# An attention and feed-forward kernel: units of three and two banks, score tiles for VectorE in a fourth row group, PV in pairs, and a finer split of the queries

## The chip, the cores and the metric

The kernel runs on one core of one Trainium2 chip. Times are device microseconds (us) of that core; a traced span is some 2 us shorter than the timed run it belongs to. The engines are called by name: TensorE (PE in the profile, with its weight loads PEld), VectorE (DVE), ScalarE (ACT), GpSimd (POOL) and SyncE (SP). There is only one core, so a "slow" state of a die cannot be told here; the runs that were timed in rounds were of the state fast, but for two of the kernel before (1024.07 and 1019.0 us), which the ratios leave out, and a kernel that was run once has the state unknown. Of those I compare stages of the trace, not the time. "Clock" is the share of its full speed that TensorE was granted: 1.00 is full, 0.50 is half ("lowered").

## The reference

One pre-norm transformer block on 2048 tokens of width 640, with 32 heads of 20, in bf16:

```python
def _A_ref(x, wqkv, wo):                      # attention
    qkv = (x @ wqkv) ... -> 3 x [B, H, S, Dh]
    scores = einsum("bhqd,bhkd->bhqk", q, k) * Dh ** -0.5
    p = softmax(scores)
    return einsum("bhqk,bhkd->bhqd", p, v) ... @ wo
def _B_ref(x, w_gate, w_up, w_down):          # feed-forward, width 1728
    return (gelu_tanh(x @ w_gate) * (x @ w_up)) @ w_down
h  = x + _A_ref(layernorm(x), wqkv, wo)
h2 = h + _B_ref(layernorm(h), w_gate, w_up, w_down)
```

The scores are 32 x 2048 x 2048 numbers. In the kernel they are 2048 tiles of 128 keys x 512 columns (512 queries of one head, or 256 queries of two key blocks), each the size of one PSUM bank. (PSUM is the memory that TensorE writes its results to; the kernel divides it into eight banks, 0 to 7.)

## The kernel before

Operations are recorded with a priority and their dependences, a small list scheduler fixes the order on each engine, and semaphores are derived from it. The order is therefore static, fixed when the program is built. Queries are handled in chunks; a "slot" is 64 tiles. The feed-forward of one chunk is background work for the attention of the next. (The code here is cut, and its comments are added.)

```python
CHUNKS = ((0, 512), (512, 512), (1024, 512), (1536, 256), (1792, 256))
D_SEL = (None, (6, 3), (6, 3), (4, 2), (4, 2))     # for VectorE: tiles per slot, and one in how many units
PV_QUADS = 1
WARM_WIN, WARM_MIN = 3.4, 0.40
...
# units of score tiles, by chunk: the banks of even and odd units
PAT = [((0, 1), (2, 3))] + [((0, 1, 2), (3, 4, 5))] * 2 + [((0, 1, 2), (3, 4))] * 2
BG  = [tuple(b for b in (7, 5, 4) if b not in PAT[c][0] + PAT[c][1]) for c in ...]   # background banks
```

A unit is two or three QK matmuls, each in its own 32-row group of TensorE, then one exponential on ScalarE over all its banks, then PV matmuls with four heads side by side in column groups ("a quad"), accumulated in bank 6. In some units of three the third tile goes to VectorE instead, which computes the exponential for a pair of tiles in integer and bf16 arithmetic:

```python
def d_exp(b, tile, prio):
    op("dve", I("tensor_scalar", v[...half...], PS[...bank...], EXP_MUL, -32000.0, ALU.mult, ALU.max), ...)
    if h == 0: return                       # wait for the second tile of the pair
    d(I("tensor_scalar", fi, v, 511, None, ALU.bitwise_and), ...)
    d(I("tensor_scalar", dw, fi, -1.0 / OCT, 1.0, ALU.mult, ALU.add), ...)
    d(I("tensor_tensor", dw, dw, fi, ALU.mult), ...)
    d(I("tensor_scalar", df, fi, -E1 / OCT, -E0, ALU.mult, ALU.add), ...)
    d(I("tensor_tensor", dw, dw, df, ALU.mult), ...)
    d(I("tensor_tensor", v, v, dw, ALU.add), ...)
    d(I("tensor_scalar", v, v, 0.25, 16256.0, ALU.mult, ALU.add), ...)
```

Where the scheduler finds TensorE idle and its use in the last 3.4 us below WARM_MIN, it puts in a matmul whose result nobody reads ("warm-up").

## Time and profile before

| | before |
|---|---|
| time, median of 3 runs | 1009.06 us (1006.16 to 1015.02) |
| traced span | 1011.4 us |
| exponentials on ScalarE | 802 for 1920 tiles; 128 tiles on VectorE |
| prologue / attention / tail | 43.3 / 925.3 / 42.8 us |
| clock 0.50 inside the attention | 8 periods, 51 us |

The lines that carry this are in the prediction below. Two things help in reading them. A row of busy time by stretch counts overlapping instructions once, so 96% for an engine says "nearly always something in flight", not "at its limit"; the limit is read from the spacing of starts. And the wait of an engine is worth something only on the path: TensorE idles before a QK because ScalarE still reads the banks (23.9 and 17.7 us in its list of waits), and that costs nothing while ScalarE sets the pace.

A bookkeeping that I use throughout: ScalarE's waits in the attention are the length of the stages, less 0.917 us for each two-bank and 1.345 us for each three-bank exponential, less the gelu interludes (9.15 us for 512 queries, 5.9 us for 256). Before, that leaves 21.3 us.

### The profile page before, as it was taken

To read this page: it belongs to the slowest core of one execution; us is meant where nothing else is said; L and a number is where in the kernel's file an instruction comes from. 1 tells how busy PE (TensorE), PEld (TensorE's weight loads), DVE (VectorE), ACT (ScalarE), POOL (GpSimd) and SP (SyncE) were. 2 spreads that over 40 slices of the span, in tenths; PEclk is the share of its full clock that TensorE was granted. 3 is DMA by queue.
4 is the path that set the end of the run, shared out by engine and by line. 5 is a ranking of instruction groups with operands and counts; after the bars stand their busy time and mean duration, and the time that the engine had idled before them with its cause. 6 is when DMAs were issued, how large, how long until landed. Compare 5 with 4: busy or idle time off the path is not lost.

```text
span 1011.4 us, 17239 instructions
## 1 busy us (share of the span) xinstructions
PE 912.7 (90%) x7392; PEld 321.1 (32%) x7392; DVE 642.6 (64%) x1319; ACT 936.9 (93%) x873; POOL 19.6 (2%) x42
## 2 busy tenths in 40 slices
PE   3999999999988788798998888889899989999988
PEld 2533322222222222222332222223333333334446
DVE  7744445555497887577669777576677645475542
ACT  3799999999999899989989999999999999999941
POOL 7000000000000000000000000000000000000000
PEclk9999999999998999899979999999999989999999
DMA  6000000000006100000010000000000000000000
GB/s 234 1 1 1 1 2 1 1 1 1 4 12 241 36 1 1 1 1 1 14 33 20 1 1 1 1 1 15 27 15 2 1 1 1 14 28 2 1 14 14
DMA packets 11820, 18.88 MB, mean 19 GB/s; under 512 B 672, under 2 KB 9824, under 8 KB 11744
## 3 DMA queue, kind: packets, MB, share of 16 engines
q1 hardware_dynamic: 11744, 17.78, 5.2%
q8 instruction: 58, 0.95, 0.4%
q14 instruction: 18, 0.15, 0.0%
HBM read 15.16 MB, written 2.62 MB: 18 GB/s over the span
## 4 chain that ended last, share of the span: by engine, by line
ACT 69%; PE 22%; DVE 6%; DMA 1%; POOL 1%; issue 1%; SPq 0%; POOLq 0%; DVEq 0%
ACT pts L305 49%; ACT rege L305 19%; PE ps L305 8%; PE ps L859 6%; PE ps L909 3%; PE ps L548 3%; DVE qt_all L305 3%; DMA rege<-in_A_wqkv_dram 1%; PE ps L512 1%; POOL regw L305 1%; DVE rege L305 1%; DVE rege L887 1%; DVE rege L898 1%; ACT L305 1%; PE ps L583 0%
## 5 line engine op out<-in xcount | busy, mean ns | idle before, releaser
L305 ACT ACTIVATE pts<-ps 128x1024 bf16<-128x1024 f32 (+1 forms) x590 | 650.3, 1354 | 13.4 <-PE ps L305 13.1
L305 PE MATMUL ps<-qt_all,kt_all 32*128 32x512 bf16 (+1 forms) x2560 | 316.2, 344 | 49.4 <-ACT pts L305 23.7
L305 ACT ACTIVATE rege<-ps 128x1536 bf16<-128x1536 f32 (+1 forms) x212 | 276.2, 1431 | 10.6 <-PE ps L305 10.3
L859 PE MATMUL ps<-rege,regw 128*128 128x512 bf16 (+2 forms) x700 | 169.8, 357 | 18.1 <-DVE rege L898 7.0
L305 PE MATMUL ps<-pts,v_all 128*21 128x512 bf16 (+1 forms) x1673 | 173.4, 350 | 0.3 <-ACT pts L305 0.2
L305 PEld LDWEIGHTS ps<-qt_all,kt_all 32*128 32x128 bf16 x2560 | 81.7, 91 | 279.2 <-ACT pts L305 164.6
L548 PE MATMUL ps<-regw 128*128 128x512 bf16 (+1 forms) x480 | 135.9, 363 | 3.2 <-DMA regw<-in_A_wqkv_dram 2.8
L305 DVE TENSOR_TENSOR qt_all<-qt_all 128x1024 bf16<-128x1024 bf16 (+1 forms) x160 | 110.0, 688 | 3.6
L305 PE MATMUL ps<-rege,v_all 128*21 128x512 bf16 (+1 forms) x807 | 99.6, 340 | 0.5 <-DVE osb L305 0.5
L859 PEld LDWEIGHTS ps<-rege,regw 128*128 128x128 bf16 (+1 forms) x700 | 59.9, 101 | 96.1 <-issue 45.5
L909 PE MATMUL ps<-regw,rege 128*128 128x320 bf16 x448 | 87.3, 307 | 1.3 <-DVE rege L877 0.8
L305 DVE TENSOR_SCALAR qt_all<-qt_all 128x1024 int16<-128x1024 int16 (+1 forms) x192 | 81.1, 422 | 4.5
L305 PEld LDWEIGHTS ps<-pts,v_all 128*21 128x21 bf16 x1673 | 43.1, 89 | 82.4 <-issue 80.5
L898 DVE TENSOR_TENSOR rege<-rege,ps 128x512 bf16<-128x512 bf16 (+1 forms) x49 | 33.6, 685 | 53.5 <-PE ps L859 53.3
L305 DVE TENSOR_SCALAR qt_all<-ps 128x512 int16<-128x512 f32 x64 | 44.0, 687 | 32.3 <-PE ps L305 32.1
L305 DVE TENSOR_SCALAR rege<-ps 128x512 int16<-128x512 f32 x64 | 43.9, 686 | 24.0 <-PE ps L305 23.5
L548 PEld LDWEIGHTS ps<-regw 128*128 128x128 bf16 x480 | 38.7, 99 | 61.8 <-issue 47.2
L909 PEld LDWEIGHTS ps<-regw,rege 128*128 128x128 bf16 x448 | 36.6, 98 | 45.9 <-issue 29.9
L887 DVE CAST rege<-ps 128x512 bf16<-128x512 f32 (+1 forms) x49 | 33.6, 686 | 22.4 <-PE ps L859 22.4
L572 DVE TENSOR_SCALAR kt_all<-ps,e 128x512 bf16<-128x512 f32 x28 | 21.0, 749 | 28.4 <-PE ps L548 28.3
L575 DVE CAST qt_all<-ps 128x512 bf16<-128x512 f32 x31 | 21.4, 689 | 25.9 <-PE ps L548 25.9
L913 DVE TENSOR_TENSOR rege<-ps,rege 128x320 bf16<-128x320 f32 x32 | 15.6, 488 | 34.0 <-PE ps L909 33.9
(78 smaller groups left out, 591.1 us busy)
## 6 DMA issues: line engine op xcount, KB each, us to landing
rege<-in_A_x_dram SPq DMA_DIRECT2D x4, 640.0 KB, 6.3
out_dram<-rege SPq DMA_DIRECT2D x16, 160.0 KB, 1.8
rege<-in_A_x_dram SPq DMA_DIRECT2D x14, 160.0 KB, 2.2
regw<-in_B_w_gate_dram SPq DMA_DIRECT2D x1, 2160.0 KB, 9.5
regw<-in_B_w_up_dram SPq DMA_DIRECT2D x1, 2160.0 KB, 14.6
regw<-in_B_w_down_dram SPq DMA_DIRECT2D x1, 2080.0 KB, 19.7
rege<-in_A_wqkv_dram SPq DMA_DIRECT2D x1, 1600.0 KB, 11.4
regw<-in_A_wqkv_dram SPq DMA_DIRECT2D x1, 800.0 KB, 13.1
```

What stands on the lines that cost most here:

```text
L305: return lambda eng: getattr(eng, method)(*args, **kwargs)
L512: op("pe", lambda eng, a=a: eng.transpose(bank16(bk, D)[:, 128 * a:128 * a + 128], src[:, a * 128:(a + 1) * 128], ident[:]), 0.055, prio, ...
L548: yield op("pe", lambda eng, l=l, r=r, k=k: eng.matmul(bank(bk, n), l, r, start=(k == 0), stop=(k == len(steps) - 1)), c_mm(n), prio, mode ...
L572: op("dve", lambda eng: eng.tensor_scalar(dst, bank(bk), e0[:, 0:1], None, ALU.add), c_dve(512) + 0.06, prio, reads=[key, "e0"], writes=[( ...
L575: op("dve", lambda eng: eng.tensor_copy(dst, bank(bk)), c_dve(512), prio, reads=[key], writes=[(nm, g, c)], rel=[bk])
L859: op("pe", lambda eng, a=a, f=f, fi=fi, mf=mf: eng.matmul(bank(bk)[0:mf, fi * nq:(fi + 1) * nq], w[:, a, f * 128:f * 128 + mf], hnT[:, a, ...
L887: cp.append(op("dve", lambda eng, bg=bg, fv=fv, m=m: eng.tensor_copy(fv, bank(bg)[0:m, :]), c_dve(512), p, reads=[kg], writes=[("ha", k)], ...
L898: hdone.append(op("dve", lambda eng, bu=bu, fv=fv, m=m: eng.tensor_tensor(fv, fv, bank(bu)[0:m, :], ALU.mult), c_dve(512), p, reads=[ku, ( ...
L909: op("pe", lambda eng, f=f, mf=mf, o=o, hf=hf, bk=bk: eng.matmul(bank(bk, 320), ha_f[0:mf, o:o + 128], wd[0:mf, f, hf * 320:(hf + 1) * 320 ...
L913: op("dve", lambda eng, bk=bk, tt=tt, hf=hf, i=i: eng.tensor_tensor(ob[:, i, hf * 320:(hf + 1) * 320], bank(bk, 320), h_sb[:, tt, hf * 320 ...
```

## The change

It aims at ScalarE, by giving VectorE more score tiles, and at TensorE, by fewer changes between its full, row-tiled and column-tiled forms. The core of the diff, cut and with comments added:

```diff
-WARM_WIN, WARM_MIN = 3.4, 0.40
+WARM_WIN, WARM_MIN = 3.4, 0.5
+PE_AGE = 1.5                      # scheduler: prefer a ready run of TensorE's present form
...
-CHUNKS = ((0, 512), (512, 512), (1024, 512), (1536, 256), (1792, 256))
+SIZES = (512, 512, 256, 256, 256, 256)
...
-PV_QUADS = 1
+PV_QUADS = 2
-PR, PR2 = 9, 6
+PR, PR2 = 12, 6
-D_SEL = (None, (6, 3), (6, 3), (4, 2), (4, 2))
+D_PER_SLOT = (4,6,8,8,8,8)
+D_FIRST, D_SPAN = 1, 16
...
-        PAT = [((0, 1), (2, 3))] + [((0, 1, 2), (3, 4, 5))] * 2 + [((0, 1, 2), (3, 4))] * 2
+        PAT = [((0, 1, 2), (3, 4))] * len(CHUNKS)
...
+            if xd:                                  # the VectorE tile of this unit
+                bd = Bank(*BG[slots[xd[0]][0]])     # a background bank, 7 or 5
+                qd = op("pe", [qk_mms(lambda: bank(bd), xd, kk) ...], 0.08,
+                        P_QK + 0.5, mode="row", ..., acq=[bd], after=[qk])
```

The rest moves buffers: the residual x is fetched straight into the accumulator tile, feed-forward buffers alternate between two halves for chunks of 256, and VectorE's scratch for chunk 0 lies in the feed-forward buffer.

## The prediction

> **What bounds the kernel now.** I read the page first, then cut the span into stages at the exponentials of each chunk of queries, then read the chain of waits for the spacing of exponentials, the timeline for the spacing of TensorE's runs, and the groups by shape for VectorE's share.
>
> The page's first part names two engines that could be the bound, and it cannot decide between them, because consecutive instructions overlap in it:
>
> ```profile
> PE 912.7 (90%) x7392; PEld 321.1 (32%) x7392; DVE 642.6 (64%) x1319; ACT 936.9 (93%) x873; POOL 19.6 (2%) x42
> ```
>
> The second view is the table of busy time by stretch. Its six rows are chunks 0 (512 queries), 1, 2 (512 each), 3, 4 (256 each) and the tail after the last exponential; after the stretch and its length come PE, PEld, DVE, ACT, POOL, the granted clock, DMA share and GB/s:
>
> ```profile
> 43.30:278.60 235.30, 234.26 (x1447) 68.64 (x1446) 115.75 (x208) 234.77 (x256) 0.00 (x0) 1.00 0.01 2
> 278.60:506.10 227.50, 193.91 (x1394) 59.43 (x1390) 170.40 (x340) 217.81 (x178) 0.00 (x0) 0.95 0.10 34
> 506.10:730.00 223.90, 195.33 (x1440) 62.49 (x1439) 162.85 (x325) 219.15 (x180) 0.00 (x0) 0.96 0.03 11
> 730.00:850.60 120.60, 113.66 (x1270) 39.87 (x1269) 77.17 (x161) 118.34 (x111) 0.00 (x0) 0.97 0.02 5
> 850.60:968.60 118.00, 113.39 (x1376) 49.18 (x1375) 67.86 (x142) 116.25 (x108) 0.00 (x0) 0.99 0.04 11
> 968.60:1011.40 42.80, 34.73 (x283) 24.61 (x279) 16.05 (x43) 8.21 (x13) 0.00 (x0) 1.00 0.04 12
> ```
>
> ScalarE is at 96 to 100% of every attention stage; VectorE has room everywhere. The true price of an exponential is its spacing in the chain, not its duration (1.23 and 1.60 us by shape):
>
> ```profile
> 43.36 209.09 ACT pts L305 x228
> ...
> 388.91 2.69 ACT rege L305 x2
> ```
>
> The first merged line is two-bank exponentials of chunk 0: 209.09/228 = 0.917 us each. The second is three-bank ones: 2.69/2 = 1.345 us. The difference, 0.428 us, is one 512-column tile; 0.917 - 2 x 0.428 = 0.061 us is the fixed cost. So merging units saves little, and taking a tile off ScalarE saves 0.428 us.
>
> The ScalarE sum for before: 1920 tiles x 0.428 + 802 exponentials x 0.061 = 821.8 + 48.9 = 870.7 us. The tanh-gelu interludes add 9.15 us for 512 queries (table load at 417.27, next exponential at 426.42) and 5.9 us for 256: 3 x 9.15 + 5.9 = 33.3. Prologue 43.3, tail 42.8. Together 990.1; the traced span is 1011.4, so 21.3 us are waits of ScalarE for TensorE, nearly all in chunks 1 to 4.
>
> Those waits sit beside a lowered clock. One of the places, in the timeline (ScalarE alone) and the table of stretches:
>
> ```profile
> 425.13 1.28 ACT L305 ACT_TABLE_LOAD   x1
> 426.42 2.37 ACT L305 ACTIVATE pts<-ps 128x1024 bf16<-128x1024 f32 x2
> 431.32 2.53 ACT L305 ACTIVATE rege<-ps 128x1536 bf16<-128x1536 f32 x2 [2.54 <-PE ps L305]
> ...
> 421.20:434.80 13.60, 11.25 (x33) 2.41 (x31) 4.48 (x8) 10.03 (x9) 0.00 (x0) 0.50 0.00 1
> ```
>
> After the gelu ScalarE waits 2.54 us for scores while TensorE runs at clock 0.50. The trace has eight such periods of 3.4 to 13.7 us inside the attention, some 51 us in all.
>
> TensorE's own price is in its starts:
>
> ```profile
> 448.12 0.82 PE L859 MATMUL ps<-rege,regw 128*128 128x512 bf16 x3
> 448.88 0.39 PE L305 MATMUL ps<-qt_all,kt_all 32*128 32x512 bf16 x3
> 449.20 0.39 PE L305 MATMUL ps<-rege,v_all 128*21 128x512 bf16 x2
> ```
>
> Three full matmuls take 0.76 us start to start, three row-tiled QK matmuls 0.32 together. With 0.215 us per 512 columns, a change between full, row-tiled and column-tiled form costs about 0.11 us, and row groups run side by side, so a fourth QK matmul in a free row group is nearly free.
>
> **What the Trainium skill says.** "TensorEngine Tiling (Array Packing)", Key Properties: changing the tiling mode drains TensorE; different tiles run in parallel. The trace agrees, at 0.11 us a change. "TensorE: Matmul & The Clock Gate", Part 1: after an idle window of about 3.4 us the clock is halved. The trace agrees in size: the lowered periods are 3.4, 6.8, 10.2 and 13.7 us at 0.50. Here partial activity is enough: in the 3.4 us before each, I count 0.19 to 0.38 of the array's columns and rows in use, against a median of 0.57. "ScalarE: Activation LUTs", What ACT_TABLE_LOAD costs: about 1283 ns per load; the trace has 1.28. "VectorE: DVE Perf Modes", Rules for kernel authors: tensor_tensor has half the top rate of scalar operations; the trace has 0.69 us against 0.42 us for 1024 elements.
>
> **The change part by part.** Counts are from the instruction order of the two built programs; durations are from the trace of before.
>
> 1. *More tiles to VectorE.* Per slot 4, 6, 8, 8, 8, 8 of 64 tiles instead of 0, 6, 6, 4, 4: 32 + 48 + 4 x 32 = 208 instead of 128. ScalarE loses 80 x 0.428 = 34.2 us.
>
> 2. *Units of 3 and 2.* 1840 tiles in 368 + 368 = 736 exponentials instead of 802: 66 x 0.061 = 4.0 us less. New sum 368 x (1.345 + 0.917) = 832.4 us. By stage: chunk 0 217.2 (was 234.8), chunk 1 209.9 (208.1), each later chunk 101.3.
>
> 3. *Six chunks instead of five.* The gelu interludes become 2 x 9.15 + 3 x 5.9 = 36.0 us: +2.7.
>
> 4. *PV by two quads and runs grouped by form.* TensorE's runs of one form fall from 2045 (783 row, 512 column, 750 full) to 1586 (730, 256, 600): 459 x 0.105 = 48 us less, plus 7 us of QK because the extra tile rides along. Warm-up matmuls grow from 52 to 119 (threshold 0.40 to 0.50), +14 us, in otherwise idle time. Summing columns and form changes, chunk 0 falls from 233 to 197 us against 217 on ScalarE, chunk 1 is 191, the later ones 91 to 100 against 101 plus 6 or 9 of gelu. TensorE is off the path, so these 41 us are not a gain; in chunk 0, where 233 stood against 235, they are what lets ScalarE's gain through.
>
> 5. *VectorE's bill.* A pair of tiles is two PSUM reads (0.69), four scalar operations (0.42) and three tensor_tensor (0.69), each some 0.085 us shorter in spacing where the next does not depend on it: about 4.6 us with the dependent ones. Forty more pairs are about 170 us. Total by stage: chunk 0 from 106 to 170 of 217, chunk 1 172 of 219, later chunks 94 to 100 of 107 to 110. VectorE goes to 87-93% there, but stays below ScalarE.
>
> 6. *Banks.* The background has banks 7 and 5 everywhere: one fewer than before in chunk 0, one more in chunks 1 and 2, the same later; the VectorE tiles now borrow them.
>
> 7. *Tail.* The changed program has 56 down-projection matmuls of the previous chunk after its last QK where before has 24; 36 of them fill the layer-norm gap that held warm-up matmuls. I put the tail at 45 us instead of 42.8.
>
> Sum: 43.3 + 832.4 + 36.0 + 45 = 956.7 us without waits.
>
> The waits are where I chose. Array use per time rises (same matmuls, shorter span) and the warm-up threshold is higher, so I expect half the lowered-clock periods and about 10 us of the 21 left. VectorE and TensorE at about 90% in four chunks, sharing two background banks, I charge with 2 us per chunk, 8 to 9 us. That is 19, or 975.7 traced. The traced run is 2.3 us above the median of the timed ones (1011.4 against 1009.06): 974.
>
> **The rivals.** *VectorE becomes the bound in the last four chunks.* For it: 94 to 100 us of chained work that must meet 107 to 110, a queue without reordering, and evictions that hold background banks. A QK matmul waiting for such a bank stops TensorE, then ScalarE. Against it: an eight-unit lag between a VectorE tile and its PV. If VectorE set the pace plus its waits, each late chunk takes 115 to 118 instead of about 110: +20 to +30 us, about 1000.
>
> *TensorE starves ScalarE through longer runs.* A double PV lasts 0.43 + 0.11 us and cannot be interrupted; after a two-bank exponential TensorE has only 0.917 us to refill three banks. For it: chunks 3 and 4 used the 3 and 2 pattern only with single PV. Against it: chunk 0 of before lost 0.5 us with TensorE 99% loaded. If one unit in four lost 0.1 us: 736/4 x 0.1 = 18 us, about 985.
>
> *The clock stays full.* If the warm-up removes nearly all lowered periods, the waits fall to about 6: 961.
>
> **Range and chances.** The ScalarE sum is firm to a few us; waits of 3 to 37 us give 958 to 992. Two per cent is 988.9, reached only if a rival takes most of its price. Faster by over 2% 0.87, within 0.11, slower 0.02.
>
> **What would show it.** Right: 736 exponentials, spaced 1.345 and 0.917 us; chunk 0 in 217 to 221 us; late chunks in 107 to 113; VectorE near 800 us busy; fewer periods at clock 0.50; ScalarE still the chain's largest part. Wrong: ScalarE's waits for scores above 35 us, chains that run through VectorE's tile arithmetic, form changes that cost more in two-quad runs, or a tail above 50 us.

## The result, and the profile after

The changed kernel took 969.89 us (median of 4 runs, 967.45 to 975.31); the kernel before took 1012.04 us in its 4 runs, three of them the earlier ones. Ratios here and below are the mean time of one kernel's fast runs over that of the other's of the same rounds, so they are not quite the ratio of the medians: 0.9595, 95% interval 0.9527 to 0.9664. Predicted were 974 us and a range of 958 to 992.

The same views of the profile after. The page's first part:

```profile
PE 862.4 (89%) x8549; PEld 352.3 (36%) x8623; DVE 798.3 (82%) x1701; ACT 901.2 (93%) x808; POOL 19.6 (2%) x42
```

VectorE went from 642.6 to 798.3 us of busy time; ScalarE fell by 36. Busy time by stretch, for the six chunks (0 and 1 of 512 queries, 2 to 5 of 256) and the tail, with the columns as before (PE, PEld, DVE, ACT, POOL, clock, DMA, GB/s):

```profile
42.70:259.60 216.90, 198.33 (x1404) 58.81 (x1427) 175.24 (x345) 216.90 (x193) 0.00 (x0) 1.00 0.00 1
259.60:479.30 219.70, 197.97 (x1463) 63.72 (x1480) 175.29 (x352) 218.82 (x194) 0.00 (x0) 0.99 0.11 37
479.30:593.90 114.60, 98.92 (x1229) 41.46 (x1243) 103.22 (x225) 111.37 (x98) 0.00 (x0) 0.99 0.01 2
593.90:696.30 102.40, 95.66 (x1262) 42.79 (x1268) 94.54 (x207) 100.73 (x90) 0.00 (x0) 1.00 0.05 15
696.30:813.30 117.00, 107.81 (x1373) 53.53 (x1373) 103.40 (x219) 114.64 (x100) 0.00 (x0) 0.97 0.03 7
813.30:922.50 109.20, 97.58 (x1309) 47.15 (x1314) 96.60 (x209) 108.20 (x95) 0.00 (x0) 0.98 0.03 8
922.50:968.50 46.00, 40.26 (x336) 29.26 (x334) 18.05 (x48) 8.16 (x13) 0.00 (x0) 0.99 0.04 15
```

ScalarE is still the fullest engine in every stage of the attention, and VectorE now follows at 80 to 92%. In chunk 0 the 192 exponentials take 216.9 us against 217.2 at their full spacing: not one wait of weight. The late chunks differ because the gelu interludes fall unevenly: none in chunk 3, two in chunk 4. The chain of waits, in two of its lines from chunk 0:

```profile
124.28 4.52 ACT pts L318 x4
128.80 2.26 ACT rege L318 x2
```

Four exponentials in 4.52 us and two in 2.26 are 2 x (1.345 + 0.917) and 1.345 + 0.917: the same price per exponential as before. TensorE with a double PV, in the timeline:

```profile
202.57 0.39 PE L726 MATMUL ps<-qt_all,kt_all 32*128 32x512 bf16 x3
202.89 0.39 PE L318 MATMUL ps<-rege,v_all 128*21 128x512 bf16 x1
202.90 0.61 PE L318 MATMUL ps<-pts,v_all 128*21 128x512 bf16 x7
203.44 0.39 PE L726 MATMUL ps<-qt_all,kt_all 32*128 32x512 bf16 x2
```

From the QK at 202.57 to the PV is 0.32 us as before; from the PV to the next QK is 0.55 us (202.89 to 203.44): two quads at 0.215 us and one change of form.

The account of the two traced spans:

| us | before | after | difference |
|---|---|---|---|
| prologue | 43.3 | 42.7 | -0.6 |
| exponentials at full spacing | 870.7 | 832.4 | -38.3 |
| gelu interludes | 33.3 | 36.0 | +2.7 |
| waits of ScalarE in the attention | 21.3 | 11.3 | -10.0 |
| tail after the last exponential | 42.8 | 46.0 | +3.2 |
| span | 1011.4 | 968.5 | -42.9 |

The rows are rounded, so the columns add up to a tenth or two. So two things paid: fewer tiles on ScalarE, as foreseen, and fewer waits, more than foreseen. The waits go with the clock: the eight periods at 0.50 (51 us) became five of 3.4 us (17 us).

### The profile page after: what moved, and what is told of

It is laid out like the page before. It is cut to its first block, busy times and chain, and to the rows that moved or that the text cites. A ratio compares the mean times of both kernels' runs of the same rounds, so it can differ in the third digit from the quotient of the medians.

```text
span 968.5 us, 19836 instructions
## 1 busy us (share of the span) xinstructions
PE 862.4 (89%) x8549; PEld 352.3 (36%) x8623; DVE 798.3 (82%) x1701; ACT 901.2 (93%) x808; POOL 19.6 (2%) x42
## 4 chain that ended last, share of the span: by engine, by line
ACT 76%; PE 16%; DVE 5%; DMA 1%; POOL 1%; issue 0%; SPq 0%; POOLq 0%; DVEq 0%
ACT pts L318 48%; ACT rege L318 26%; PE ps L896 5%; PE ps L954 4%; PE ps L726 4%; PE ps L318 2%; DVE qt_all L318 2%; DMA rege<-in_A_wqkv_dram 1%; PE ps L561 1%; ACT L318 1%; ACT regw L531 1%; POOL regw L318 1%; DVE rege L686 0%; DVE qt_all L686 0%; PE ps L525 0%
## 5 line engine op out<-in xcount | busy, mean ns | idle before, releaser
L318 ACT ACTIVATE pts<-ps 128x1536 bf16<-128x1536 f32 x492 | 587.0, 1375 | 10.5 <-PE ps L726 6.5
L726 PE MATMUL ps<-qt_all,kt_all 32*128 32x256 bf16 (+1 forms) x3072 | 307.8, 312 | 61.9 <-ACT pts L318 35.2
L318 ACT ACTIVATE rege<-ps 128x1536 bf16<-128x1536 f32 x244 | 305.7, 1376 | 2.9 <-PE ps L726 2.5
L896 PE MATMUL ps<-rege,regw 128*128 128x256 bf16 (+3 forms) x820 | 150.0, 312 | 9.4 <-ACT rege L318 4.3
L318 DVE TENSOR_TENSOR qt_all<-qt_all 128x1024 bf16<-128x1024 bf16 (+1 forms) x220 | 150.6, 685 | 3.3
L318 PE MATMUL ps<-pts,v_all 128*21 128x256 bf16 (+1 forms) x1830 | 136.6, 313 | 0.0
L318 DVE TENSOR_SCALAR qt_all<-qt_all 128x1024 bf16<-128x1024 int16 (+1 forms) x264 | 107.5, 418 | 2.3
L686 DVE TENSOR_SCALAR rege<-ps 128x512 int16<-128x512 f32 x120 | 82.4, 686 | 32.8 <-PE ps L726 32.2
L318 PE MATMUL ps<-rege,v_all 128*21 128x256 bf16 (+1 forms) x1090 | 106.5, 313 | 0.0
L318 DVE TENSOR_SCALAR rege<-rege 128x1024 int16<-128x1024 int16 (+1 forms) x108 | 45.1, 418 | 0.7
## 6 DMA issues: line engine op xcount, KB each, us to landing
regw<-in_B_w_up_dram SPq DMA_DIRECT2D x1, 2160.0 KB, 14.4
rege<-in_A_wqkv_dram SPq DMA_DIRECT2D x1, 1600.0 KB, 11.3
```

Of the source, the lines that this page charges most:

```text
L318: return lambda eng: getattr(eng, method)(*args, **kwargs)
L686: d_ops.append(op("dve", lambda eng: eng.tensor_scalar(v[:, 512 * h:512 * h + 512], bank(b), EXP_MUL, -32000.0, ALU.mult, ALU.max), c_dve( ...
L726: return lambda eng: eng.matmul(out()[:, kk * nq:(kk + 1) * nq], kt_all[32 * j:32 * j + 32, g, kt * 128:(kt + 1) * 128], qt_all[32 * j:32 ...
L896: op("pe", lambda eng, a=a, f=f, fi=fi, mf=mf: eng.matmul(bank(bk)[0:mf, fi * nq:(fi + 1) * nq], w[:, a, f * 128:f * 128 + mf], hnT[:, a, ...
```

## The experiments

My theory is the prediction's: ScalarE sets the pace, the tiles are the main gain, the lowered clock makes most waits. The main rivals are that TensorE's form changes or its warm-up are the real gain, and that VectorE is already the next bound. All twelve ran on the changed kernel with a small edit, except one on the kernel before and one repeat.

### The 80 tiles back on ScalarE

```diff
-D_PER_SLOT = (4,6,8,8,8,8)
+D_PER_SLOT = (4,4,4,4,4,4)
```

> The changed kernel with 4 VectorE tiles in every slot: 128 in all, as many as before the change; everything else of the change stays. My theory (ScalarE's sum sets the pace, so the gain is the 80 tiles): 768 exponentials, 384 x (1.345 + 0.917) = 868.6 us instead of 832.4, so about 36 us longer than the changed kernel, 1003 to 1010 us; that is nearly all of the gain given back, though TensorE keeps its fewer changes of form. Rival (the gain comes from TensorE: fewer changes of form, double PV, more warm-up matmuls): it stays within 12 us of the changed kernel, under 982 us.

Measured: 999.52 us (998.67 to 1004.61), ratio to before 0.9876 (0.9807 to 0.9946). The tiles thus carry 0.9876 - 0.9595 = 0.028 of the 0.0405 gained, about 28 us. (Against the 0.963 of the repeat below it is 0.025 of 0.037.) That is far from the rival, but 3.5 us below the lower edge of my own expectation. Two stages of its profile:

```profile
606.50:721.30 114.80, 107.01 (x1378) 51.07 (x1384) 66.80 (x142) 114.72 (x102) 0.00 (x0) 1.00 0.07 19
...
953.00:996.90 43.90, 34.53 (x277) 24.47 (x278) 15.11 (x41) 8.35 (x13) 0.00 (x0) 0.96 0.03 8
```

Chunk 3 has 96 exponentials (108.6 us) and one gelu interlude (5.9): 114.5 of 114.8 us, so practically no wait, with VectorE at 58%. Summed over the attention the waits are 6.5 us instead of 11.3, and the tail is 43.9 us instead of 46.0. Giving the 80 tiles to VectorE takes 36.2 us off ScalarE, and with it come 4.8 us more of waits and 2.1 us more of tail. That their load on VectorE and the background causes these is likely and not shown: the two traces of the changed kernel (below) differ from each other by 3.1 and 1.8 us.

With 128 tiles this kernel is still 11 to 14 us faster than the one before, and in the traces that is all waits: 6.5 us against 21.3, while the exponentials and interludes sum to nearly the same. The finer split of the queries and the moved buffers were not tested by themselves.

### PV of one quad

```diff
-PV_QUADS = 2
+PV_QUADS = 1
```

> The changed kernel with PV of one quad at a time. TensorE's runs rise from 1586 to 1931, some 36 us more of form changes in its sum (7 in each 512 chunk, about 4 in each late one). My theory (TensorE is off the path): 0 to 6 us longer, 969 to 976 us, with chunk 0 at 217 us as now. Rival A (form changes are on the path): 20 us or more longer, 990 us. Rival B (the long double PV starves ScalarE): shorter than the changed kernel by 3 us or more.

Measured: 972.59 us (972.23 to 974.37), ratio 0.9603 (0.954 to 0.9667): 2.7 us above the changed kernel's median, which is within the noise (the repeat below has 972.90). Both rivals fall. One detail is against my theory, though: chunk 0 took 222.0 us, not 217. The timeline at the start of a slot:

```profile
153.53 0.74 DVE L608 SCALAR_TENSOR_TENSOR qt_all<-ps,khalf,qt_all 128x512 bf16<-128x512 f32 x1
...
153.67 1.04 PE L561 MATMUL ps<-regw 128*128 128x512 bf16 x4 [1.10 <-DVE o_nat L840]
...
154.64 0.60 PE L726 MATMUL ps<-qt_all,kt_all 32*128 32x512 bf16 x6
155.08 2.37 ACT L318 ACTIVATE pts<-ps 128x1536 bf16<-128x1536 f32 x2 [4.79 <-PE ps L726]
```

ScalarE waits 4.79 us for the first scores of the next heads, because their query projection was finished by VectorE only at 154.27 and TensorE then had a run of another projection to end before it could start the scores at 154.64. The likely reading is that with more form changes TensorE's background work in chunk 0 runs late, and at a slot's border background becomes path. The tail also grew, from 46.0 to 54.9 us, because the last gelu interlude and more of the feed-forward fell into it, while the late chunks got shorter. So TensorE's savings are not worth their 36 us; in chunk 0 they may be worth 5, by one trace.

### Chunk 0 in its old form

```diff
-        PAT = [((0, 1, 2), (3, 4))] * len(CHUNKS)
+        PAT = [((0, 1), (2, 3))] + [((0, 1, 2), (3, 4))] * (len(CHUNKS) - 1)
-PV_QUADS = 2
+PV_QUADS = 1
```

> The single-PV kernel with units of two banks in chunk 0, as before the change. TensorE's sum in chunk 0 is 220 us (204 with units of 3 and 2, 197 in the changed kernel), ScalarE's 240 x 0.917 = 220 us. If the TensorE saving was needed to let ScalarE's gain through, chunk 0 takes 226 us or more; if TensorE keeps up at 100% load as it did before, 220 to 223 us.

Measured in one run: chunk 0 took 224.1 us, between the two expectations (979.45 us in all). ScalarE's 240 exponentials need 220.1 us; 3.7 of the 4 us above it are one wait, at 157 us, of the same kind as in the single-PV kernel. So TensorE's saving is worth some 7 us in chunk 0 (224.1 against 216.9), 3 of which are ScalarE's own smaller sum. The prediction had let the whole gain of that chunk (235.3 to 216.9) depend on it. The test does not bring back the whole old load, though: by the counts TensorE's sum is 220 us here and was 233 in the kernel before.

### No preference for the present form

```diff
-PE_AGE = 1.5
+PE_AGE = -1.0
```

> The changed kernel with the choice of a run of the same form switched off in the scheduler. Its instruction order has 1573 runs against 1586, so I expect no difference: span 964 to 974 us, chunk 0 at 217 us. It shows that the fall from 2045 runs comes from double PV and the larger units alone, which the prediction had lumped together with this choice. Rival (the choice avoids waits): 980 us or more.

Measured in one run: span 962.6 us, chunk 0 217.8 us. The preference brings nothing that can be seen; the one time, 964.36 us, even lies below all ten of the changed kernel (967.45 to 975.31), but it is one run. By counts of the programs' orders the 459 runs saved come from double PV (345: with single PV there are 1931 runs, with double PV 1586) and, the other 114, from the larger units.

### No warm-up matmuls

```diff
-WARM_WIN, WARM_MIN = 3.4, 0.5
+WARM_WIN, WARM_MIN = 3.4, 0.0
```

> The changed kernel without warm-up matmuls (119 of them away). My theory (low array use in a window of 3.4 us halves the clock, and the halved clock is what makes ScalarE wait): the periods at clock 0.50 inside the attention rise from 5 (17 us in all) to 8 to 14 (30 to 60 us), waits of ScalarE from 11 us to 18 to 30, time 977 to 990 us. Rival (the warm-up matmuls do nothing, or cost as much as they save): within 4 us of the changed kernel, lowered periods no more than 7.

Measured: 986.70 us (983.3 to 989.28), ratio 0.9737 (0.9669 to 0.9806), 17 us above the changed kernel. Eleven periods at clock 0.50, 123 us in all, twice what I had allowed; waits 24.3 us. Chunk 2, by stretch, and ScalarE alone in the timeline inside it:

```profile
481.70:593.50 111.80, 98.40 (x1172) 38.56 (x1181) 99.21 (x218) 103.69 (x91) 0.00 (x0) 0.81 0.01 2
```

```profile
517.56 2.37 ACT L318 ACTIVATE rege<-ps 128x1536 bf16<-128x1536 f32 x2 [0.15 <-PE ps L726]
521.17 2.37 ACT L318 ACTIVATE pts<-ps 128x1536 bf16<-128x1536 f32 x2 [1.24 <-PE ps L726]
523.91 1.45 ACT L318 ACTIVATE pts<-ps 128x1536 bf16<-128x1536 f32 x1 [0.38 <-PE ps L726]
525.84 1.02 ACT L318 ACTIVATE pts<-ps 128x1024 bf16<-128x1024 f32 x1 [0.47 <-PE ps L726]
```

The mean clock is 0.81, and between 513.7 and 527.4 us, where the trace has it at 0.50, ScalarE waits for scores again and again. Much of the lowered time costs nothing: 123 us at half speed gave 13 us more of waits, most likely because TensorE has slack.

### The warm-up threshold alone, on the kernel before

```diff
-WARM_WIN, WARM_MIN = 3.4, 0.40
+WARM_WIN, WARM_MIN = 3.4, 0.50
```

> The kernel before with the warm-up threshold of the change alone (0.40 to 0.50). My theory: lowered-clock time falls from 51 us to 15 to 35 us, ScalarE's waits from 21 to 10 to 16 us, so 4 to 10 us faster than before, ratio 0.990 to 0.996. Rival (the shorter span, not the threshold, removed the lowered periods): ratio 0.998 to 1.002, lowered time still 45 us or more.

Measured: 1006.40 us (1003.77 to 1010.5) against 1010.59, ratio 0.9947 with an interval of 0.9864 to 1.003: not clear of no change. In the trace, chunk 1, which had 227.5 us at a mean clock of 0.95:

```profile
278.90:502.30 223.40, 182.52 (x1375) 58.79 (x1389) 170.56 (x340) 217.29 (x178) 0.00 (x0) 0.99 0.10 34
```

Lowered time inside the attention is 14 us instead of 51, waits are 11.2 us instead of 21.3, and the span is 1002.0 us. But this is the luckiest of four runs. The record gives each run's mean clock, and with it the lowered time, 2 x (1 - clock) x span: about 14, 40, 48 and 30 us here (mean 33), 34 to 82 us in the seven runs of the kernel before in the same rounds (mean 56), and a later run of the kernel before, at 1003.72 us, had 14 us too. So the threshold alone probably takes away part of the lowered time, without a shorter span; how much is not shown.

### A still higher threshold

```diff
-WARM_WIN, WARM_MIN = 3.4, 0.5
+WARM_WIN, WARM_MIN = 3.4, 0.60
```

> The changed kernel with the warm-up threshold at 0.60 instead of 0.50, 138 warm-up matmuls instead of 119. If lowered-clock time is still costing something, it falls from 17 us to under 8 us and ScalarE's waits from 11 to 6 to 9 us: 964 to 968 us. Rival (what is left are waits of ordinary ordering, and more warm-up matmuls stand in the way): 969 to 974 us.

Measured: 968.14 us (966.9 to 969.99), ratio 0.9583 (0.9532 to 0.9635). Lowered time 10 us, waits 7.6 us, span 965.1. The waits are as expected, the lowered time is not quite (under 8 us was expected); the time lies between the two expectations and within the changed kernel's noise, so this is no version that beats it.

### 32 more tiles for VectorE

```diff
-D_PER_SLOT = (4,6,8,8,8,8)
+D_PER_SLOT = (6,8,8,8,8,8)
```

> The changed kernel with 6, 8, 8, 8, 8, 8 VectorE tiles per slot: 240 in all, 32 more. ScalarE's exponentials sum to 362 x 1.345 + 361 x 0.917 = 817.9 us, 14.5 less. VectorE's sum rises to 200 us of 210 in chunk 0 and to 204 of 203 + 9 in chunk 1. Theory 1 (ScalarE still sets the pace): 952 to 958 us. Theory 2 (VectorE at 95% or more, and the background work that it and two banks push back, become waits and a longer tail): 964 to 976 us, with chunk 0 or 1 well above ScalarE's sum or a tail above 50 us. I lean to theory 2.

Measured: 988.58 us (984.7 to 991.84), ratio 0.9783 (0.9711 to 0.9856): 19 us slower than the changed kernel, and 12 us beyond what even theory 2 allowed. Theory 1 falls. Chunk 0, with 7.8 us less on ScalarE (209.4 against 217.2) than in the changed kernel, took 9 us longer (226.0 against 216.9):

```profile
42.80:268.80 226.00, 207.50 (x1407) 60.16 (x1407) 201.30 (x408) 210.70 (x186) 0.00 (x0) 0.96 0.00 1
```

The chain of waits through its longest stop, at a slot's border:

```profile
157.09 1.27 PE ps L561 x5
...
158.38 0.76 DVE kt_all L585
...
159.19 1.04 PE ps L561 x4
160.23 0.35 PE ps L726 x3
...
160.60 1.45 ACT pts L318
```

The path runs through projections on TensorE and, on VectorE, the copies of their results out of PSUM; ScalarE stands 4.9 us. The clock is lowered for 61 us in the whole attention, and the tail is 57.6 us.

### More tiles in chunk 0 alone

```diff
-D_PER_SLOT = (4,6,8,8,8,8)
+D_PER_SLOT = (6,6,8,8,8,8)
```

> The changed kernel with 6 VectorE tiles per slot in chunk 0 instead of 4, nothing else: 464 tiles for ScalarE there, 209.4 us at full rate; VectorE 200 us. In the 240-tile kernel chunk 0 took 226.0 us. If chunk 0's own load is the cause, it takes 222 to 228 us again, and chunk 1, with 6 tiles as in the changed kernel, about 220 us.

The result was wrong (relative error 0.23). The edit makes the list of tiles overshoot its end by one (a VectorE tile is counted into an odd remainder), so the loop that emits units skips the last one: the program has 2047 of 2048 score tiles, and the last PVs are missing. Chunk 0 does not depend on that. It took 219.5 us, against 209.4 of ScalarE's sum; my expectation of 222 to 228 was missed, since in the 240-tile kernel the same chunk took 226.0. The difference goes with the clock, 1.00 here and 0.96 there (17 us at 0.50): the three longest stops, 3.25, 1.9 and 5.2 us, are in both, and the other stops of the 240-tile kernel lie in its lowered periods or within 2 us after them. Chunk 1 took about 223 us, with 10 us of lowered clock; about 220 was expected.

### The same, with a third background bank

```diff
-        PAT = [((0, 1, 2), (3, 4))] * len(CHUNKS)
+        PAT = [((0, 1), (2, 3))] + [((0, 1, 2), (3, 4))] * (len(CHUNKS) - 1)
-D_PER_SLOT = (4,6,8,8,8,8)
+D_PER_SLOT = (6,6,8,8,8,8)
```

> The same 6 tiles per slot in chunk 0, with units of two banks there, which frees a third background bank (7, 5, 4). VectorE's sum in chunk 0 stays at 198 us, TensorE's is 206, ScalarE's 232 x 0.917 = 212.7 us. If the two background banks are what loses time in the 224-tile kernel, chunk 0 takes 213 to 217 us. If VectorE's load is, it takes 222 us or more.

The result was correct, 971.01 us in one run. Chunk 0 with two background banks (first) and with three, each kernel by stretch:

```profile
42.70:262.20 219.50, 195.16 (x1384) 59.63 (x1407) 200.68 (x408) 209.86 (x185) 0.00 (x0) 1.00 0.00 1
```

```profile
42.50:259.50 217.00, 208.47 (x1384) 61.14 (x1408) 200.24 (x411) 213.49 (x233) 0.00 (x0) 1.00 0.00 1
```

VectorE does the same 200 us of work in both. With two banks 10.1 us are lost over ScalarE's sum, with three 4.3 (217.0 against 212.7), at the upper edge of what the bank theory expected. More than half of the loss so seems to be the borrowed bank, and the rest stays; this edit also changes the unit size, so it is not a clean separation, and VectorE's share is not settled.

### A try at beating both, and the changed kernel again

The try has WARM_MIN 0.60, PE_AGE -1.0, and

```diff
-D_FIRST, D_SPAN = 1, 16
+D_FIRST, D_SPAN = 0, 16
```

> A try at beating both: the changed kernel with warm-up threshold 0.60, the choice of a run of the same form off, and VectorE tiles from the first unit of a slot on instead of the second. ScalarE's sum is the same 832.4 us; lowered-clock time should stay under 12 us and waits at 5 to 9 us: 962 to 967 us, against 969.9 for the changed kernel. If waits are ordinary scheduling noise: 967 to 972 us, no gain.

> The changed kernel itself, for the same rounds as the tuned one: 967 to 973 us, ratio 0.955 to 0.965.

Measured over five rounds and a profiled run: the try 978.38 us (977.02 to 979.58), ratio 0.9697 (0.9666 to 0.9728); the changed kernel 972.90 us (967.46 to 974.95), ratio 0.963 (0.959 to 0.967). The try lost, outside both of its expectations. Its trace has 65 us at clock 0.50 in eleven periods and 22.3 us of waits, although the threshold is the higher one; the scheduler put in only 94 warm-up matmuls. That is no chance: all six runs had a mean clock of 0.967 to 0.974. Which of the three edits did it was not tested; two of them alone (the threshold, no preference) had 10 us of lowered clock each, so the earlier start of VectorE's tiles, alone or with them, is what is left. The repeat of the changed kernel had 27 us of lowered clock, 14.4 us of waits and a 47.8 us tail in its trace (span 973.1), against 17, 11.3 and 46.0 in the first. One program, so this is chance from run to run.

No kernel tried was shown to beat the changed one.

## Why the prediction was right

The traced sum was 956.7 us without waits; the trace has 957.2 (968.5 less 11.3). By its own steps:

1. *More tiles to VectorE, and units of 3 and 2.* Right: 736 exponentials at 0.917 and 1.345 us, 832.4 us. Giving the 80 tiles back cost 25 to 28 us in time: in the traces 36.2 us on ScalarE, less 4.8 of waits, 2.1 of tail and 0.8 of prologue.
2. *Gelu interludes.* Right in sum: 36.0 us. They fall unevenly, though, so that of the late chunks, foreseen at 107 to 113 us, only one lies there (114.6, 102.4, 117.0 and 109.2 us; the mean is 110.8).
3. *TensorE's form changes.* The count was right, the reading half so. It named double PV and grouping together; grouping brought nothing, in one run. It called TensorE off the path; with single PV the time is 2.7 us longer, within the noise; in its trace chunk 0 loses 5 us and the tail 9, which late chunks win back. Its claim that the saving in chunk 0 lets the gain through holds for 4 to 7 of 18 us: the old form of that chunk is 7.2 us longer (224.1 against 216.9), of which 3 is ScalarE's own larger sum.
4. *VectorE.* Foreseen near 800 us busy and 87 to 93% in the late chunks; measured 798.3 us, 88 to 92%. It did not become the bound in the changed kernel. (The bill had a slip: 40 pairs at 4.6 us are 184, not 170; busy time grew by 155.7.) One step further, 32 more tiles in chunks 0 and 1, cost 19 us. That is not the rival as it was written, which spoke of the last four chunks and of VectorE's arithmetic: the loss was in chunks 0 and 1 (some 17 and 12 us of waits) and in the tail, with projections on the path, probably the borrowed banks, and 61 us of lowered clock.
5. *Banks.* Mentioned and not priced. With 6 tiles per slot in chunk 0, where two background banks serve projections and VectorE tiles, a third bank took away some 6 of 10 us lost, in a test that also changed the unit size; with the 4 tiles of the change nothing is lost (216.9 us).
6. *Tail.* 45 foreseen, 46.0 and 47.8 measured.
7. *Waits.* The term that was mis-sized: 10 us for the clock and 8 to 9 for the load, 19 in all; 11.3 and 14.4 measured. I had expected half the lowered periods to stay; a third of the time did in the first trace and half in the second, and half by the mean clocks of all runs (24 us of 46). The load took less than I charged: the two variants with all 208 tiles and 10 us of lowered clock had 7.6 and 7.0 us of waits in all, hardly more than the 6.5 of the kernel with 128 tiles. A finer split is not shown. There is luck in the 974: I took 2.3 us off the traced sum of 975.7, because the traced run of before (1013.19 us) was slower than the median. That of the changed kernel was an ordinary one, with a span 1.4 us below the median. So in the trace the forecast was 7.2 us too high, and only in the timed median 4 us (1 us in the second).

The waits beside the time at clock 0.50 inside the attention, in the traces:

| kernel | lowered, us | waits, us |
|---|---|---|
| no preference for a form | 10 | 7.0 |
| threshold 0.60 | 10 | 7.6 |
| 128 tiles | 14 | 6.5 |
| before, threshold 0.50 | 14 | 11.2 |
| PV of one quad | 14 | 11.8 |
| changed | 17 | 11.3 |
| chunk 0 in its old form | 17 | 13.8 |
| changed, again | 27 | 14.4 |
| 224 tiles, third bank | 27 | 16.2 |
| before | 51 | 21.3 |
| 240 tiles | 61 | 38.1 |
| the try | 65 | 22.3 |
| 224 tiles (wrong result) | 66 | 30.5 |
| no warm-up | 123 | 24.3 |

The removal of the warm-up shows that lowered time brings waits; the size per us is not constant, and waits from other causes are in the column, most of all with 224 and 240 tiles. The runs of one program say more than the single traces. By their mean clocks the 23 fast runs of the kernel before in the experiments' rounds had 14 to 82 us of lowered time (mean 46), and the 10 of the changed one 14 to 37 (mean 24). A straight line through each set gives 0.28 and 0.32 us of time per us lowered. An estimate from this: the 22 us less are worth 6 to 7 of the 40 us gained, beside the tiles.

## What to carry to other kernels

Price an engine's work by the spacing of its starts, add the interludes, and what is left over is waits: here that sum was within 1 us of the trace, and all the uncertainty lay in the waits. When work moves to an idle engine, the gain is the moved time less what the new load gives back. With 32 tiles more it gave back through other work's deadline (projections at the border of a slot) and, it seems, the buffers it borrowed, with that engine 89% busy in chunk 0. Where an array is kept at its full clock by activity, look at the clock of each stage before explaining a wait, and run the same program twice.

## What the Trainium skill lacked or had wrong

- "TensorE: Matmul & The Clock Gate", Part 1: its table puts the lowering after an idle window; a later passage says that micro-idles between groups of matmuls bring it too, without a figure. Here a window of 3.4 us with 0.19 to 0.38 of the array in use was enough (before; 0.28 to 0.34 in the changed kernel). The page says that the window runs freely, and all fourteen traces agree: in each, the lowered periods start and end on one grid of 3.41 us, to 0.01 us, and the place of the grid against the kernel differs from trace to trace. What it lacks is how much use is too little. Inside the attention 87 windows of these grids at full clock were followed by a lowering, each with at most 0.41 of the array in use; of the 3090 windows with more, none was. (A matmul counts as 0.215 us per 512 columns, times the share of the array's row and column groups that it uses.) Where the grid falls is the likely reason why one program had 17 us at clock 0.50 inside the attention in one trace and 27 in another.
- The same page names a warm-up for benchmarks, and otherwise the avoiding of idle gaps; that warm-up matmuls in the gaps of a kernel are a means is not on it. Without them lowered time rose to 123 us and the kernel took 17 us longer.
- The same page, Part 1: it says that recovery takes one busy window. With no warm-up two periods lasted 27.3 us while TensorE worked at 0.16 to 0.38 of the array's use in windows of 3.4 us, so a window used that little did not end them.
- "TensorEngine Tiling (Array Packing)", Key Properties: it gives no figure for the drain between tiling modes; the runs show 0.11 us.
- "ScalarE: Activation LUTs", What ACT_TABLE_LOAD costs: it puts a switch at about 2.66 us, load and drain together. In the trace of before a load of 1.28 us starts 0.02 us after the recorded end of the last exponential (417.25) and the gelu starts 0.01 us after it (418.56): no separate drain of over a microsecond is seen.
- "TensorE: Matmul & The Clock Gate", Terms: it puts the penalty at the lowered time times (1 - K/N), which is half of it at clock 0.50. Here, where TensorE is not the bound, it was less: 0.28 us per us from run to run of the kernel before, and 106 us more of lowered time without warm-up made 13 us of waits.
